# A linear-attention and mixture kernel: head work placed by a mask, key sums 64 columns wide, queries and first products in halves

## The chip, the cores and the metric

The kernel runs on one core of a Trainium2 chip. The metric is the device time of one execution in microseconds (us), the median over several runs. The engines are named as in the profile: PE is TensorE, PEld its weight loads, DVE VectorE, ACT ScalarE, POOL GpSimd, SP the engine that issues most DMAs.

## What is computed

Attention with a quadratic feature map, then a gated feed-forward (`_moe_ref`), then a soft mixture of 8 experts (`_moe2_ref`). The changed places serve the first two.

```python
def phi(x):                                   # S1, S2: 8 x 32
    a = np.einsum('rd,bhsd->bhsr', S1, x)
    b = np.einsum('rd,bhsd->bhsr', S2, x)
    return np.einsum('bhsi,bhsj->bhsij', a, b).reshape(*x.shape[:-1], r * r)
q_p, k_p = (phi(q), phi(k))                   # q, k, v: 4 x 4 x 1088 x 32
kv = np.einsum('bhsf,bhsd->bhfd', k_p, v)
z = np.sum(k_p, axis=2)
num = np.einsum('bhsf,bhfd->bhsd', q_p, kv)
den = np.einsum('bhsf,bhf->bhs', q_p, z)[..., None] + 1e-06
...
xn = x / rms * rms_g                          # 4352 tokens of 128
g = xn @ w_gate                               # 128 x 1536
val = xn @ w_val
return (silu * val @ w_out).astype(np.float32)
```

S1, S2 and the feed-forward weights arrive as 8-byte numbers. Each is made into a 4-byte word on the chip from its two halves (`f64_words`: two ACT passes, two DVE passes, one integer add).

## The kernel before

The tokens are worked off in nine tiles: tiles 0 to 7 hold 512 tokens, two for each batch, tile 8 the last 64 rows of all batches. For each tile the feed-forward runs through twelve slots (T, f), one for each 128 of the 1536 hidden columns. A slot's `ff_in` forms gate and value by three products each: high part of x by high part of the weight, high by low, low by high (`mm3`, lines 646 to 650), 512 tokens wide. ACT takes the silu of the gate (line 677), DVE multiplies it with the value (line 678), and two slots later `ff_out` adds the result to the tile's output. In tile 0 this last product uses whole 4-byte words (line 702), later tiles split words.

Before the first slot stands the head, which makes the sums of batch 0 and the x of tile 0. Its order is written out by hand in the string `FRONT` (lines 29 to 35), one token for one step; each engine keeps the order of the string. The tokens that matter here:

- `n:18` issues 18 products on constant data that nothing reads (line 301).
- `b` is `make_bd`: S1 and S2 become words, one PE transpose puts them on 128 partitions, and four ACT copies lay them into `bd`, a 128 x 64 block matrix with a 32 x 16 block for each head.
- `kt:g`, `kp:g`, `kx:g`, `ko:g` transpose the keys, multiply them with `bd`, copy one half of the result and form the outer products; `kv:hp` copies the values of two heads into `va`, 33 columns for each head and slice (32 values and a one).
- `ks:hp` sums outer products with values for the heads 2hp and 2hp+1 (line 389): 18 products with a stationary operand of 33 columns, the first head's at output partition 0, the second's at 64.
- `kw:hp` copies that sum to `kvT` (line 407, one copy for each head), `kb:hp` transposes it back, `kl:f` puts it in place (line 434).
- `qs`, `qp`, `qh`, `qo`, `qb`, `qa`, `qd` and so on do the same for the queries of tile 0; `qx` writes the high part of x (line 601), `ql` the low part (line 607).
- `c:i` is the next step of weight conversion i; i = 0, 1, 3, 4 hold gate and value columns for slots 0-1, 2-3, 4-5 and 6-7, i = 2 and 5 output weights. Line 192 and line 198 are its ACT passes, line 204 its add on POOL, line 242 the cast to the high part on ACT, line 249 the low part on POOL.

After the head the conversions go on beside the slots of tile 0. Batches 1 to 3 get their sums by `k_chain`, a step or two in each slot; the same line 389 works there. A scheduler that models the engines' times sets the order of the instructions from the first slots on, so any change in the head can reorder the rest. DMAs stand on SP's queue in the order in which the code issues them.

Of the kernel before, what the change touches and what calls it, by code (L numbers as in the profile page):

```python
# [8 lines left out]
F32 = mybir.dt.float32  # L9
F32R = mybir.dt.float32r  # L10
# [6 lines left out]
P = 128  # L17
# [13 lines left out]
FRONT = """  # L31
n:18 b n:5 kz kt:0 kt:1 qs kp:0 kp:1 kt:2 kx:0:a ko:0:d kx:1:b ko:1:p kc:2 qp kp:2 n:3 kv:0 kx:2:a ko:2:d qh kv:1 km
ks:0 c:0 qo:0 qo:1 qb c:0 c:0 ks:1 kw:0:a kb:0 kw:1:a n:4 kb:1 n:10 kl:0:a kl:1:d c:0 c:0 kr:a c:1
qa:0 qa:1 n:26 qd:0 qd:1 c:0 qq:0:a qq:1:d qq:2:a qq:3:d qr:0 qr:1 c:1 qm:0 qm:1 c:1 c:0 qt:0 qx:0 n:2 qt:1 qx:1 c:1 ql c:1 c:2 c:2 c:2
# [13 lines left out]
def body(ctx, tc, q, k, v, s1, s2, wg, wv, wo, rg, phi, w1, w2, out):  # L48
# [38 lines left out]
    kt, qt, kr, vt = {}, {}, {}, {}  # L87
    va = const.tile([P, H, 8, D1], F32, name="va")
    vr = const.tile([64, H, D1], F32, name="vr")

# [22 lines left out]
    def load_q(b):  # L113

        t = big("qt", 2)
        load(out=t.rearrange("p (h n) -> p h n", h=H), in_=q[b, :, 0:1024, :].rearrange("h (p j) d -> p h (j d)", j=8))
        qt[b] = t.rearrange("p (h j d) -> p h j d", h=H, j=8)

    stage = {}

# [18 lines left out]
    load_k(0)  # L139
    load_q(0)  # L140
    load_kr(0)
    load_v(0)
    load_w(w_keys[0])
    load_w(w_keys[1])
    g_sb = const.tile([P, 1], F32, name="g_sb")
# [18 lines left out]
    pool.memset(vr[:, :, D:D1], 1.0)  # L164
    mhalf = const.tile([P, 4], F32, name="mhalf")
# [20 lines left out]
    def f64_words(st, t, s, r, out):  # L186
# [14 lines left out]
        yield  # L201
        if len(out.shape) == 2:
            for c in cuts(out.shape[1]):
                mark["word"] = pool.tensor_tensor(out=out[:, c], in0=s[:, c], in1=r[:, c], op=ALU.add).ins
        else:
            s, r = (x.unsqueeze(1).to_broadcast(out.shape) for x in (s, r))
            pool.tensor_tensor(out=out, in0=s, in1=r, op=ALU.add)
        yield
# [51 lines left out]
    def make_bd():  # L260
        w = sb.tile([2 * R, D], F32, tag="cst", name="cst")
        s = sb.tile([2 * R, D], U32, tag="css", name="css")
        r = sb.tile([2 * R, D], U32, tag="csc", name="csc")
        w4 = sb.tile([2 * R, 4, D], F32, tag="csr", name="csr")
        for _ in f64_words(s64, w, s, r, w4.bitcast(U32)):
# [53 lines left out]
    class Keys:  # L319
# [58 lines left out]
        def sum(self, hp, ts, banks=1):  # L378

            for t in ts:  # L380
# [112 lines left out]
    class Queries:  # L493
# [389 lines left out]
    def front():  # L883
# [375 lines left out]
```

## Time and profile before

| What | us |
|---|---|
| Median of 3 runs (314.46 to 315.02) | 314.61 |
| Profiled execution, its own time | 314.55 |
| Span from first to last instruction | 312.8 |
| Part of its own time outside the span | 1.75 |
| PE busy | 303.6 |
| DVE busy | 234.5 |
| ACT busy | 181.7 |
| POOL busy | 63.4 |

The page of the profile gives busy time by engine and in 40 slices of 7.8 us. Finer questions are put to the trace: a timeline lists instructions in order of time, with the engine's idle time before one in brackets and what ended it, and windows give each engine's busy time in chosen stretches. Matmul records are pipelined and overlap; their durations are longer than the step from one to the next. The granted TensorE clock is 1.00 of full speed (2.4 GHz) in the stretches before 300 us.

### The profile page before, as it was taken

The page shows a single profiled execution, that of the slowest core. Times are in us where ns is not written, and L with a number is a line of the kernel's source. Part 1 is how long each engine was busy: PE and PEld are TensorE (multiplying, and loading weights), DVE is VectorE, ACT ScalarE, POOL GpSimd, SP SyncE. Part 2 cuts the span into 40 slices and gives each one's busy share as a digit, 9 for nine tenths or more (in the row PEclk, how much of TensorE's full clock was granted, in tenths as well). Part 3 has the DMA queues.
Part 4 walks back from the last instruction along what each step waited for, and adds up shares of the span by engine and source line. Part 5 has one row for each costly group of instructions (what it writes and reads, how often), then busy time and mean ns, then how long its engine had stood idle before and what let it go on. Part 6 is the DMA issues. An engine that isn't in the chain of part 4 may idle for free.

```text
span 312.8 us, 5555 instructions
## 1 busy us (share of the span) xinstructions
PE 303.6 (97%) x1977; PEld 241.8 (77%) x1977; DVE 234.5 (75%) x458; ACT 181.7 (58%) x411; POOL 63.4 (20%) x104
## 2 busy tenths in 40 slices
PE   8989999999999999999999999999999999999993
PEld 6776666778887878888888788888787778898482
DVE  4787967688789858967898689678787667666762
ACT  3768664455745467565544676555574655566552
POOL 3357998000612010020020100100020100003120
PEclk9999999999999999999999999999999999999999
DMA  8988000010035100010351000100891494000007
GB/s 204 311 300 216 0 0 1 11 25 2 0 112 111 25 2 0 11 25 0 91 130 25 3 0 9 26 0 10 290 266 26 129 303 106 2 0 2 3 32 254
DMA packets 44955, 23.97 MB, mean 77 GB/s; under 512 B 26880, under 2 KB 40960, under 8 KB 44928
## 3 DMA queue, kind: packets, MB, share of 16 engines
q1 hardware_dynamic: 44752, 23.56, 28.1%
q8 instruction: 15, 0.25, 0.3%
q10 hardware_dynamic: 176, 0.07, 0.1%
q14 instruction: 12, 0.10, 0.1%
HBM read 19.81 MB, written 2.23 MB: 70 GB/s over the span
## 4 chain that ended last, share of the span: by engine, by line
PE 87%; DVE 4%; SPq 2%; POOL 2%; ACT 2%; DMA 1%; issue 1%; DVEq 0%; POOLq 0%; ACTq 0%
PE v L647 8%; PE g L647 8%; PE g L649 8%; PE g L648 8%; PE v L648 7%; PE v L649 7%; PE o L649 7%; PE o L647 7%; PE o L648 7%; PE aux L534 4%; PE o L702 3%; PE aux L389 2%; SPq L76 2%; PE aux L359 2%; PE aux L511 2%; PE fo L1210 1%
## 5 line engine op out<-in xcount | busy, mean ns | idle before, releaser
L677 ACT ACTIVATE silu<-g 128x512 f32<-128x512 f32 (+1 forms) x103 | 60.5, 592 | 38.7 <-PE g L649 38.1
L687 ACT CAST hh<-hf 128x512 fp32r<-128x512 f32 x89 | 54.9, 617 | 44.4 <-DVE hf L678 42.8
L678 DVE TENSOR_TENSOR hf<-v,silu 128x512 f32<-128x512 f32 (+1 forms) x91 | 61.2, 677 | 23.4 <-ACT hh L687 7.8
L692 DVE TENSOR_TENSOR hl<-hf,hh 128x512 fp32r<-128x512 f32 x89 | 60.5, 682 | 13.6 <-ACT hh L687 12.6
L647 PE MATMUL g<-xh,wgh 128*128 128x512 f32 (+1 forms) x108 | 43.8, 407 | 1.0 <-ACT xh L601 0.6
L647 PE MATMUL v<-xh,wgh 128*128 128x512 f32 (+1 forms) x108 | 43.4, 402 | 0.0
L648 PE MATMUL g<-xh,wgl 128*128 128x512 f32 (+1 forms) x108 | 41.1, 380 | 0.5 <-POOL wgl L249 0.5
L649 PE MATMUL g<-xl,wgh 128*128 128x512 f32 (+1 forms) x108 | 41.5, 384 | 0.0
L648 PE MATMUL v<-xh,wgl 128*128 128x512 f32 (+1 forms) x108 | 41.4, 383 | 0.0
L649 PE MATMUL v<-xl,wgh 128*128 128x512 f32 (+1 forms) x108 | 40.9, 379 | 0.0
L647 PE MATMUL o<-hh,woh 128*128 128x512 f32 (+1 forms) x94 | 36.9, 393 | 0.0
L649 PE MATMUL o<-hl,woh 128*128 128x512 f32 (+1 forms) x94 | 36.8, 392 | 0.0
L648 PE MATMUL o<-hh,wol 128*128 128x512 f32 (+1 forms) x94 | 35.8, 381 | 0.0
L582 POOL TENSOR_SCALAR rs<-ss 128x4 f32<-128x4 f32 (+1 forms) x8 | 1.9, 241 | 142.9 <-ACT sq L575 142.9
L647 PEld LDWEIGHTS g<-xh,wgh 128*128 128x128 f32 x108 | 20.3, 188 | 6.6 <-ACT silu L677 1.5
L648 PEld LDWEIGHTS g<-xh,wgl 128*128 128x128 f32 x108 | 20.3, 188 | 4.9 <-POOL wgl L249 0.9
L647 PEld LDWEIGHTS v<-xh,wgh 128*128 128x128 f32 x108 | 20.4, 188 | 4.3 <-issue 1.1
L649 PEld LDWEIGHTS g<-xl,wgh 128*128 128x128 f32 x108 | 20.3, 188 | 4.0
L649 PEld LDWEIGHTS v<-xl,wgh 128*128 128x128 f32 x108 | 20.3, 188 | 4.0 <-issue 0.2
L648 PEld LDWEIGHTS v<-xh,wgl 128*128 128x128 f32 x108 | 20.4, 188 | 3.9 <-issue 0.7
L649 PEld LDWEIGHTS o<-hl,woh 128*128 128x128 f32 x94 | 17.7, 188 | 3.7 <-issue 0.8
L647 PEld LDWEIGHTS o<-hh,woh 128*128 128x128 f32 x94 | 17.7, 188 | 3.4 <-issue 0.4
(259 smaller groups left out, 510.7 us busy)
## 6 DMA issues: line engine op xcount, KB each, us to landing
ring<-in_moe_w_dram SPq DMA_DIRECT2D x12, 256.0 KB, 7.3
ring<-in_moe_w_dram SPq DMA_DIRECT2D x5, 512.0 KB, 5.3
ring<-in_k_dram SPq DMA_DIRECT2D x8, 256.0 KB, 2.9
qt<-in_q_dram SPq DMA_DIRECT2D x4, 512.0 KB, 5.3
ring<-in_v_dram SPq DMA_DIRECT2D x16, 128.0 KB, 4.6
ring<-in_moe_w_gate_dram SPq DMA_DIRECT2D x6, 256.0 KB, 6.3
ring<-in_moe_w_val_dram SPq DMA_DIRECT2D x6, 256.0 KB, 7.7
ring<-in_moe_w_out_dram SPq DMA_DIRECT2D x3, 512.0 KB, 7.1
```

Source lines behind the costliest of these rows:

```text
L76: i = (on or nc.sync).dma_start(out=out, in_=in_)
L359: pe.matmul(o, self.kT[g][:, P * t : P * t + pp], bdf, start=True, stop=True)
L389: pe.matmul(self.a["kv", hp][64 * h2 : 64 * h2 + D1, 64 * hp : 64 * hp + 64], va[:, h, 2 * i + g, :] if t < 8 else vr[:, h, :], self.pk[hp ...
L534: pe.matmul(o, pD[:, f, h, :], rhs, start=(f == 0), stop=(f == 1))
L647: first = pe.matmul(o, ah, bh, start=start, stop=False)
L648: pe.matmul(o, al, bh, start=False, stop=False)
L649: last = pe.matmul(o, ah, bl, start=False, stop=stop)
L677: mark["silu"] = act.activation(s[:, cs], g[:, cs], AF.Silu).ins
L678: mark["gate"] = mark["gate", T, f] = dve.tensor_tensor(out=hf32[T, f][:, cs], in0=v[:, cs], in1=s[:, cs], op=ALU.mult).ins
L687: act.copy(hh[T, f], hf32[T, f])
L692: dve.tensor_tensor(out=hl[T, f], in0=hf32.pop((T, f)), in1=hh[T, f].bitcast(F32), op=ALU.subtract)
L702: last = pe.matmul(ops[T][:, 0:w], w_c, h[:, cs], start=(c == 0), stop=(c == NF - 1))
```

## The change

In the head, four things are done otherwise, and `FRONT` is rewritten.

1. S is added up on DVE instead of POOL, and 16 x 32 instead of 16 x 128. Four small products put it on 128 partitions, and one DVE multiply with a mask `blk` lays it into `bd`. The four ACT copies and the transpose go.
2. The stationary operand of the sums is 64 columns wide instead of 33, so that it runs into the columns of the next slice or head. `kvT` is then written in one copy of 97 partitions for a pair of heads instead of two of 33. This holds for all batches.
3. Tile 0's queries are loaded by a DMA of their own, half as large; the other half follows behind the first pair of weights.
4. The first slot, (0, 0), forms its high products for tokens 0 to 255 first and 256 to 511 after.

```diff
 FRONT = """
-n:18 b n:5 kz kt:0 kt:1 qs kp:0 kp:1 ... kp:2 n:3 kv:0 kx:2:a ko:2:d qh kv:1 km
-ks:0 c:0 qo:0 qo:1 qb c:0 c:0 ks:1 kw:0:a kb:0 kw:1:a n:4 kb:1 n:10 kl:0:a kl:1:d c:0 c:0 kr:a c:1
+n:17 b n:5 kz kt:0 bm kt:1 qs kp:0 kp:1 ... kp:2 kv:0 kx:2:a ko:2:d qh kv:1 km
+ks:0 qo:0 qo:1 qb ks:1 kw:0:a c:0 c:0 kb:0 kw:1:a n:2 kb:1 n:10 kl:0:a kl:1:d c:0 c:0 c:0 kr:a c:1
...
@@ load_q
+        src = q[b, :, 0:1024, :].rearrange("h (p j) d -> p h (j d)", j=8)
+        if b > 0:
+            load(out=t, in_=src)
+        else:
+            q0 = row("hl", 3, F32R).bitcast(F32)
+            load(out=q0.rearrange("p (h n) -> p h n", h=H), in_=src[:, :, 0 : 4 * D])
+            q0s.append(q0)
+            return lambda: load(out=t[:, :, 4 * D :], in_=src[:, :, 4 * D :])
...
-    load_q(0)
+    rest_q = load_q(0)
     load_kr(0)
     load_v(0)
     load_w(w_keys[0])
+    rest_q()
     load_w(w_keys[1])
...
-    pool.memset(bd, 0.0)
+    blk = const.tile([P, H], F32, name="blk")
+    pool.memset(blk, 0.0)
+    for h in range(H):
+        pool.memset(blk[32 * h : 32 * h + 32, h : h + 1], 1.0)
...
-    pool.memset(kvT[32:64], 0.0)
...
@@ f64_words
+        if out.shape[1] == D:
+            dve.tensor_tensor(out=out, in0=s, in1=r, op=ALU.add)
...
@@ make_bd
-        pe.transpose(a[:, 0 : 2 * R], w4.rearrange("p h d -> p (h d)"), ident[0 : 2 * R, 0 : 2 * R])
-        for h in range(4):
-            act.copy(bd[32 * h : 32 * h + 32, h, :], a[32 * h : 32 * h + 32, 0 : 2 * R])
+        for h in range(H):
+            pe.matmul(a[32 * h : 32 * h + 32, 0 : 2 * R], w, ident[0 : 2 * R, 0 : 2 * R], start=True, stop=True)
+        kt["S"] = a
+
+    def place_bd():
+        a = kt.pop("S")[:, 0 : 2 * R].unsqueeze(1).to_broadcast([P, H, 2 * R])
+        dve.tensor_tensor(out=bd, in0=a, in1=blk.unsqueeze(2).to_broadcast([P, H, 2 * R]), op=ALU.mult)
...
@@ Keys.sum
+                    v0 = D1 * (8 * h + 2 * i + g) if t < 8 else D1 * h
                     pe.matmul(
-                        self.a["kv", hp][64 * h2 : 64 * h2 + D1, 64 * hp : 64 * hp + 64],
-                        va[:, h, 2 * i + g, :] if t < 8 else vr[:, h, :],
+                        self.a["kv", hp][64 * h2 : 64 * h2 + 64, 64 * hp : 64 * hp + 64],
+                        (va_all if t < 8 else vr_all)[:, v0 : v0 + 64],
...
@@ Keys.spread_1
-            for h2 in range(2):
-                r0 = 64 * h2
-                src = self.a["kv", hp][r0 : r0 + D1, 64 * hp : 64 * hp + 64].rearrange("p (a n) -> p a n", n=D)
-                eng(kvT[r0 : r0 + D1, 2 * hp : 2 * hp + 2], src.unsqueeze(2).to_broadcast([D1, 2, 4, D]))
+            src = self.a["kv", hp][0:97, 64 * hp : 64 * hp + 64].rearrange("p (a n) -> p a n", n=D)
+            eng(kvT[:, 2 * hp : 2 * hp + 2], src.unsqueeze(2).to_broadcast([97, 2, 4, D]))
...
@@ ff_in
+        if (T, f) == (0, 0):
+            os, sl = (gps[T, f][0], vps[T, f][0]), slice(0, P)
+            for cs in cuts(512):
+                for w_m in (wgh, wgl):
+                    for m, o in enumerate(os):
+                        last = pe.matmul(o[:, cs], w_m[:, m, sl], xh[T][:, cs], start=(w_m is wgh and cs.start == 0), stop=False)
+                        gate[0] = gate[0] or last.ins.name
+            for m, o in enumerate(os):
+                last = pe.matmul(o, wgh[:, m, sl], xl[T], start=False, stop=True)
+            mark["mm3"] = last.ins
+            return
```

`va_all` and `vr_all` are `va` and `vr` with 31 more columns, which POOL sets to zero; POOL also sets the mask, and no longer `bd` and the middle of `kvT`.

On DVE, at the start of the program, this stood between the words of S (`cst`, `css`) and the first outer products (`work`); `T` holds transposed keys, `x_192` the transposed queries:

```order
L194 TENSOR_SCALAR cst<-cst 16x32
L200 SCALAR_TENSOR_TENSOR css<-s_64,cst 16x32
L341 STREAM_TRANSPOSE T<-ring 128x2x4x32 x4
L506 STREAM_TRANSPOSE x_192<-qt 128x512
L287 TENSOR_TENSOR work<-asb,aux 128x1024
```

Now the add of S (a program's own instruction, shown as ISA, over 64 half words) and the multiply with the mask stand there too:

```order
L210 TENSOR_SCALAR cst<-cst 16x32
L216 SCALAR_TENSOR_TENSOR css<-s_64,cst 16x32
L219 ISA cst<-css,csc 16x64
L359 STREAM_TRANSPOSE T<-ring 128x2x4x32 x2
L288 TENSOR_TENSOR bd<-aux,blk 128x64
L359 STREAM_TRANSPOSE T<-ring 128x2x4x32 x2
L523 STREAM_TRANSPOSE x_198<-hl 128x512
L305 TENSOR_TENSOR work<-asb,aux 128x1024
```

The multiply has two of the four key transposes ahead of it and two behind.

On ACT, from the x of tile 0 on, the order was this; `silu_435`, `silu_465` and `silu_495` are the silus of slots 0, 1 and 2, `wgh<-cvt_321` is the cast of the gate and value columns for slots 2 and 3, and `hf`, `cvc` and `ring_407` belong to later conversions:

```order
L601 ACTIVATE xh_393<-v_398,g_sb_88 128x256
L192 ACTIVATE ring_407<-ring_90 128x512
L198 ACTIVATE cvc_409<-ring_90 128x512
L242 CAST wgh_133<-cvt_321 128x2x256
L677 ACTIVATE silu_435<-g_414 128x512
L192 ACTIVATE hf_445<-ring_92 128x512
L198 ACTIVATE cvc_447<-ring_92 128x512
L192 ACTIVATE hf_476<-ring_95 128x512
L677 ACTIVATE silu_465<-g_457 128x512
L677 ACTIVATE silu_495<-g_487 128x512
```

Now the same stretch reads so; `silu_438`, `silu_468` and `silu_498` are the silus of slots 0, 1 and 2, `wgh<-cvt_320` the cast for slots 2 and 3:

```order
L618 ACTIVATE xh_392<-v_397,g_sb_90 128x256
L208 ACTIVATE ring_406<-ring_92 128x512
L214 ACTIVATE cvc_408<-ring_92 128x512
L705 ACTIVATE silu_438<-g_413 128x512
L208 ACTIVATE hf_448<-ring_94 128x512
L208 ACTIVATE hf_479<-ring_97 128x512
L257 CAST wgh_141<-cvt_320 128x2x256
L214 ACTIVATE cvc_450<-ring_94 128x512
L705 ACTIVATE silu_468<-g_460 128x512
L214 ACTIVATE cvc_481<-ring_97 128x512
L300 COPY asb_484<-aux_455 128x128
L257 CAST wgh_141<-hf_448 128x2x256
```

The cast for slots 2 and 3 stood ahead of the first silu; it now stands behind that silu and two more passes.

On PE, slots 1 and 2 stood like this (`g_457` and `v_458` are slot 1, `g_487` and `v_488` slot 2):

```order
L647 MATMUL v_458<-xh_393,wgh_133 128x512
L648 MATMUL v_458<-xh_393,wgl_134 128x512
L649 MATMUL v_458<-xl_394,wgh_133 128x512
L647 MATMUL g_487<-xh_393,wgh_133 128x512
L648 MATMUL g_487<-xh_393,wgl_134 128x512
L649 MATMUL g_487<-xl_394,wgh_133 128x512
L647 MATMUL v_488<-xh_393,wgh_133 128x512
L648 MATMUL v_488<-xh_393,wgl_134 128x512
L649 MATMUL v_488<-xl_394,wgh_133 128x512
```

Now (`g_460`, `v_461` slot 1; `g_490`, `v_491` slot 2; `o_510` the tile's output):

```order
L664 MATMUL v_461<-xh_392,wgh_141 128x512
L665 MATMUL v_461<-xh_392,wgl_142 128x512
L666 MATMUL v_461<-xl_393,wgh_141 128x512
L664 MATMUL g_490<-xh_392,wgh_141 128x512
L664 MATMUL v_491<-xh_392,wgh_141 128x512
L730 MATMUL o_510<-hh_439,ring_406 128x512
```

Slot 2's products with the low weights now come later, behind the output products of slots 0 and 1.

## Rows read from the trace of the kernel before

**Rows 1.** The page, busy time of each engine (us, share of span, instructions):

```profile
PE 303.6 (97%) x1977; PEld 241.8 (77%) x1977; DVE 234.5 (75%) x458; ACT 181.7 (58%) x411; POOL 63.4 (20%) x104
```

**Rows 2.** Windows: length, then busy PE, PEld, DVE, ACT, POOL (instructions), clock, DMA:

```profile
22.06:25.10 3.04, 3.01 (x12) 2.17 (x12) 1.27 (x4) 2.22 (x5) 2.07 (x3) 1.00 0.33 98
25.10:27.28 2.18, 1.75 (x6) 0.97 (x6) 2.17 (x4) 2.18 (x5) 1.55 (x3) 1.00 0.88 278
27.28:33.60 6.32, 5.82 (x23) 3.64 (x23) 6.32 (x11) 4.79 (x10) 5.58 (x8) 1.00 0.62 136
33.60:42.55 8.95, 8.94 (x43) 6.81 (x44) 8.23 (x15) 6.03 (x11) 8.95 (x10) 1.00 0.00 0
100.00:150.00 50.00, 50.00 (x323) 40.67 (x322) 39.07 (x73) 28.95 (x68) 3.54 (x5) 1.00 0.07 11
```

**Rows 3.** Timeline, 4 to 7.7 us: start, us, instruction, [idle before <-releaser]:

```profile
4.34 0.18 DVE L200 SCALAR_TENSOR_TENSOR css<-s,cst 16x32 uint32<-16x32 uint32 x1
4.45 2.00 DVE L341 STREAM_TRANSPOSE T<-ring 128x256 f32<-128x256 f32 x4
4.67 0.44 POOL L207 TENSOR_TENSOR csr<-css,csc 16x128 uint32<-16x128 uint32 x1 [2.25 <-DVE css L200]
5.17 0.23 PE L268 MATMUL aux<-ident,csr 16*128 16x16 f32 x1
5.44 0.69 ACT L270 COPY bd<-aux 32x16 f32<-32x16 f32 x4 [1.22 <-PE aux L268]
6.18 1.10 PE L359 MATMUL aux<-bd,T 128*128 128x64 f32 x8
6.75 0.71 DVE L506 STREAM_TRANSPOSE x<-qt 128x512 f32<-128x512 f32 x1 [0.30 <-DMA qt<-in_q_dram]
```

**Rows 4.** Timeline, 9 to 14.2 us, key sums and their copies:

```profile
9.35 0.19 PEld L359 LDWEIGHTS g<-bd,T 128*64 128x64 f32 x2
9.61 0.50 PE L301 MATMUL idle<-hot 128*128 128x256 bf16 x3
9.95 0.62 ACT L352 COPY va<-ring 128x512 f32<-128x512 f32 x1
10.04 1.09 PE L389 MATMUL v<-work,va 128*33 128x64 f32 x32
12.31 0.30 PE L389 MATMUL aux<-pkr,vr 64*33 64x64 f32 x4
12.80 0.74 ACT L407 COPY kvT<-aux 33x256 f32<-33x256 f32 x2
13.60 0.30 PE L417 MATMUL aux<-ident,kvT 97*128 97x97 f32 x1
```

**Rows 5.** PE's weight loads, 239.87 to 239.90 us, where they are 64 columns wide:

```profile
239.88 0.15 PEld L541 LDWEIGHTS aux<-kvr,work 128*64 128x64 f32 x2 [0.35 <-issue]
```

**Rows 6.** Timeline, 21 to 27.4 us, the first slots:

```profile
21.54 0.48 ACT L601 ACTIVATE xh<-v,g_sb 128x256 fp32r<-128x256 f32 x1 [0.20 <-PE v L594]
22.07 0.50 PE L647 MATMUL g<-xh,wgh 128*128 128x512 f32 x1 [0.57 <-ACT xh L601]
22.30 1.63 POOL L204 TENSOR_TENSOR cvt<-cvs,cvc 128x256 uint32<-128x256 uint32 x2 [1.81 <-DVE cvs L200]
23.56 0.39 PE L649 MATMUL g<-xl,wgh 128*128 128x512 f32 x1
23.96 0.62 ACT L242 CAST wgh<-cvt 128x512 fp32r<-128x512 f32 x1 [0.82 <-POOL cvt L204]
24.48 0.59 ACT L677 ACTIVATE silu<-g 128x512 f32<-128x512 f32 x1
24.98 0.65 ACT L192 ACTIVATE hf<-ring 128x512 f32<-128x512 f32 x1
25.13 0.50 PE L647 MATMUL g<-xh,wgh 128*128 128x512 f32 x1
```

**Rows 7.** PE's timeline at 42.5 us, the first product of slot 8:

```profile
42.56 0.79 PE L647 MATMUL g<-xh,wgh 128*128 128x512 f32 x1
```

More of the change, by code (lines that the diff above doesn't have):

```diff
@@ L31 @@
 FRONT = """
-n:18 b n:5 kz kt:0 kt:1 qs kp:0 kp:1 kt:2 kx:0:a ko:0:d kx:1:b ko:1:p kc:2 qp kp:2 n:3 kv:0 kx:2:a ko:2:d qh kv:1 km
-ks:0 c:0 qo:0 qo:1 qb c:0 c:0 ks:1 kw:0:a kb:0 kw:1:a n:4 kb:1 n:10 kl:0:a kl:1:d c:0 c:0 kr:a c:1
+n:17 b n:5 kz kt:0 bm kt:1 qs kp:0 kp:1 kt:2 kx:0:a ko:0:d kx:1:b ko:1:p kc:2 qp kp:2 kv:0 kx:2:a ko:2:d qh kv:1 km
+ks:0 qo:0 qo:1 qb ks:1 kw:0:a c:0 c:0 kb:0 kw:1:a n:2 kb:1 n:10 kl:0:a kl:1:d c:0 c:0 c:0 kr:a c:1
 qa:0 qa:1 n:26 qd:0 qd:1 c:0 qq:0:a qq:1:d qq:2:a qq:3:d qr:0 qr:1 c:1 qm:0 qm:1 c:1 c:0 qt:0 qx:0 n:2 qt:1 qx:1 c:1 ql c:1 c:2 c:2 c:2
@@ L87, in body @@
     kt, qt, kr, vt = {}, {}, {}, {}
-    va = const.tile([P, H, 8, D1], F32, name="va")
-    vr = const.tile([64, H, D1], F32, name="vr")
+    va_all = const.tile([P, H * 8 * D1 + 31], F32, name="va")
+    vr_all = const.tile([64, H * D1 + 31], F32, name="vr")
+    va = va_all[:, 0 : H * 8 * D1].rearrange("p (h j d) -> p h j d", h=H, d=D1)
+    vr = vr_all[:, 0 : H * D1].rearrange("p (h d) -> p h d", d=D1)
     def load_k(b):
@@ L115, in load_q @@
         t = big("qt", 2)
-        load(out=t.rearrange("p (h n) -> p h n", h=H), in_=q[b, :, 0:1024, :].rearrange("h (p j) d -> p h (j d)", j=8))
         qt[b] = t.rearrange("p (h j d) -> p h j d", h=H, j=8)
+        src = q[b, :, 0:1024, :].rearrange("h (p j) d -> p h (j d)", j=8)
+        t = t.rearrange("p (h n) -> p h n", h=H)
+        if b > 0:
[5 more added lines that the diff above has]
+            return lambda: load(out=t[:, :, 4 * D :], in_=src[:, :, 4 * D :])
+    q0s = []
     stage = {}
@@ L161, in body @@
     bd = const.tile([P, H, 2 * R], F32, name="bd")
-    pool.memset(bd, 0.0)
+    blk = const.tile([P, H], F32, name="blk")
+    pool.memset(blk, 0.0)
+    for h in range(H):
+        pool.memset(blk[32 * h : 32 * h + 32, h : h + 1], 1.0)
     pool.memset(va[:, :, :, D:D1], 1.0)
     pool.memset(vr[:, :, D:D1], 1.0)
+    pool.memset(va_all[:, H * 8 * D1 :], 0.0)
+    pool.memset(vr_all[:, H * D1 :], 0.0)
     mhalf = const.tile([P, 4], F32, name="mhalf")
@@ L201, in f64_words @@
         yield
-        if len(out.shape) == 2:
+        if out.shape[1] == D:
+            dve.tensor_tensor(out=out, in0=s, in1=r, op=ALU.add)
+        else:
             for c in cuts(out.shape[1]):
                 mark["word"] = pool.tensor_tensor(out=out[:, c], in0=s[:, c], in1=r[:, c], op=ALU.add).ins
-        else:
-            s, r = (x.unsqueeze(1).to_broadcast(out.shape) for x in (s, r))
-            pool.tensor_tensor(out=out, in0=s, in1=r, op=ALU.add)
         yield
@@ L263, in make_bd @@
         r = sb.tile([2 * R, D], U32, tag="csc", name="csc")
-        w4 = sb.tile([2 * R, 4, D], F32, tag="csr", name="csr")
-        for _ in f64_words(s64, w, s, r, w4.bitcast(U32)):
+        for _ in f64_words(s64, w, s, r, w.bitcast(U32)):
             pass
         a = aux()
-        pe.transpose(a[:, 0 : 2 * R], w4.rearrange("p h d -> p (h d)"), ident[0 : 2 * R, 0 : 2 * R])
-        for h in range(4):
-            act.copy(bd[32 * h : 32 * h + 32, h, :], a[32 * h : 32 * h + 32, 0 : 2 * R])
+        for h in range(H):
[4 more added lines that the diff above has]
+        dve.tensor_tensor(out=bd, in0=a, in1=blk.unsqueeze(2).to_broadcast([P, H, 2 * R]), op=ALU.mult)
     bdf = bd.rearrange("p h r -> p (h r)")
@@ L397, in spread @@
         def spread(self):
-            for h2 in range(2):
-                r0 = 64 * h2
-                src = self.a["kv"][r0 : r0 + D1, 0:128].rearrange("p (a n) -> p a n", n=D)
-                act.copy(kvT[r0 : r0 + D1], src.unsqueeze(2).to_broadcast([D1, 4, 4, D]))
+            src = self.a["kv"][0:97, 0:128].rearrange("p (a n) -> p a n", n=D)
+            act.copy(kvT, src.unsqueeze(2).to_broadcast([97, 4, 4, D]))
         def spread_1(self, hp, eng):
-            for h2 in range(2):
-                r0 = 64 * h2
-                src = self.a["kv", hp][r0 : r0 + D1, 64 * hp : 64 * hp + 64].rearrange("p (a n) -> p a n", n=D)
-                eng(kvT[r0 : r0 + D1, 2 * hp : 2 * hp + 2], src.unsqueeze(2).to_broadcast([D1, 2, 4, D]))
+            src = self.a["kv", hp][0:97, 64 * hp : 64 * hp + 64].rearrange("p (a n) -> p a n", n=D)
+            eng(kvT[:, 2 * hp : 2 * hp + 2], src.unsqueeze(2).to_broadcast([97, 2, 4, D]))
         def back(self, ids=range(4), banks=1):
@@ L501, in shuffle @@
             self.qD = row("T", 2) if T else row("x2")
-            if T < 8:
+            if T == 0:
+                src = q0s[0]
+            elif T < 8:
                 src = qt[T // 2][:, :, 4 * (T % 2) : 4 * (T % 2) + 4, :].rearrange("p h j d -> p h (j d)")
@@ L893, in front @@
             "b": make_bd,
+            "bm": place_bd,
             "kz": k.zero,
```

## The prediction

> **What bounds the kernel now.** I read the page first: PE is busy for 97% of the span [rows 1]. Next come windows of the trace. In the steady part, 100 to 150 us, PE has no idle time at all, while DVE and ACT have a fifth or more of theirs free [rows 2]. So an edit that only relieves DVE, ACT or POOL there gives nothing; what counts is when PE's stream of slots begins, how much PE waits before it is closed up, and the length of PE's own work. The windows of the first slots show where it waits: 0.03, 0.43, 0.50 and 0.01 us from 22.06 to 42.55 us, 0.97 together, and nothing after [rows 2]. Last I read the timelines of the head and of the first slots, following what each instruction waited for [rows 3, 4, 6]. The head is a chain that passes through all engines: S, key projections, key sums, `kvT`, back transposes, queries, x of tile 0, first product at 22.07. The 1.75 us of the execution outside its span I leave as they are, so gains are taken from the profiled execution's 314.55; it lies 0.06 below the median of the runs, which is nothing at this size.
>
> **S and the mask.** Before, DVE's last word step ends at 4.52, POOL adds until 5.11, PE transposes, four ACT copies take 5.44 to 6.13, and the first projection starts at 6.18 [rows 3]. After, DVE adds by itself. No row shows that instruction; the step before it, 16 x 32, took 0.18 and POOL's add 0.44 [rows 3], so I bound it by these and take 0.2, since it has 64 columns on the engine of the 0.18. It ends at 4.75. PE's four small products follow in about 0.4 (the transpose took 0.23) beside two key transposes on DVE, half of the 2.00 for four; DVE starts each next instruction about 0.07 before the last ends (4.45 against 4.52) [rows 3], so they end near 5.7. Then the multiply: 64 columns from PSUM, not shown either; between 0.18 and the 0.69 of the four copies that it replaces, I take 0.22, nearer the single instruction. With 0.05 from the last copy to PE, as before, the first projection starts at 5.95, 0.23 earlier. With 0.44 and 0.69 it would start 0.5 later than this, 0.25 after the old time. What stands behind the multiply on DVE are two key transposes and that of the queries. The second half of the keys is wanted a projection later and is there in time. The queries' transpose waited 0.30 for its DMA [rows 3]; with half the bytes in front of it that wait goes, and it pays for the 0.42 of the two new DVE instructions. The outer products of the keys thus start about 0.1 earlier, and PE's projections, which run back to back, 0.23 earlier.
>
> The POOL memsets and SP's one more DMA issue cost nothing that I can find: POOL has 2 us free before 4.67 [rows 3]. The second half of the queries stands in SP's queue ahead of the second pair of weights and all later ones, but the bytes ahead of these are the same as before, and an issue takes under half a us; only tile 1 wants that half. If the cover failed, the cost would be that issue.
>
> **Key sums.** Before, three idle products stand at 9.61 and the first sum starts at 10.04 [rows 4]. Without them it starts behind the last projection (9.35 less 0.23), at about 9.28. A new wait appears: the last slice of head 1, read 64 columns wide, runs into the first slice of head 2, which the second `va` copy writes. That copy ended at 10.57 [rows 4] and ends near 10.35 now; the last products of the first sum wait 0.25 for it, and behind them on PE stand the rest of this sum and the second one. Both sums took from 10.04 to 12.61 [rows 4], so now 9.28 + 2.57 + 0.25 = 12.10. Then `kvT`: two copies ended at 13.54, at 0.37 each and behind two conversion passes on ACT [rows 4]. One copy of the same columns ends at 12.5, and one of the passes has moved behind the next placing copies. The second back transpose starts at 12.56 instead of 13.60: **1.04 earlier**. Placing, attend, divide and x follow in the same order with the same waits, so I carry 1.04 to the first slot. The moved ACT pass runs while DVE still prepares the other operand of POOL's add.
>
> Width costs PE itself nothing if the two heads' loads still run side by side. The sums' step is 1.09 less one record for 32, 56 ns for a pair [rows 4]. Elsewhere in this trace two 64-wide loads at different output partitions take 0.15 together, against 0.19 for two in one place [rows 4, 5], so they overlap and the load hides under the product. I take 0. The other end is no overlap at all, a pair taking twice its step, 56 ns more: 18 pairs in each of eight sums (two in each batch), 1.0 us a sum, 8 in all. A page of the Trainium skill leans that way: "TensorE: Matmul & The Clock Gate", section LDWEIGHTS, has a load's time grow with its columns, by its rate an estimate of 27 ns for 33 columns and 53 for 64, so 107 for two one after another. Against it, "TensorEngine Tiling (Array Packing)", Key Properties, has tiles load and multiply in parallel; the 64-wide loads here agree with that, 0.15 for two.
>
> **First slot.** PE waited 0.57 for the second half of x [rows 6]. Now four half products, 256 columns, fit into that gap. A product takes about 0.25 (12 in 3.01) [rows 2]; I cost a half at 0.12, bounded by 0.25 if halving saved nothing, which would cost 0.5 more. Lead of PE at the end of slot 1: 1.04 + 0.46 = **1.5**, at about 23.55 instead of 25.08.
>
> **What is given back.** This is the step that I trust least and that decides. Slot 2's gate needs the cast of its weights on ACT. Before, that cast stood ahead of the first silu, and PE went on at 25.13 with almost no stop [rows 6]. Now it stands behind the first silu and two passes. The silu waits for the low product of the gate (23.56 less 1.5, plus 0.4 for its run): 22.5. From the silu's start to the next pass is 0.50 [rows 6], the two passes take about 0.55 each, the cast 0.62: done at 24.75, PE at 24.8. PE has run out at 23.55 and stands for 1.25. The lead falls to 0.33. But the work that before stood behind later waits now comes first: two high products, an output product, the projection for tile 1. Of the old waits, 0.43 and 0.50, I find about 0.15 (the first output product waits for POOL's add, which waits for the multiply of slot 0) and 0.25 (slot 4's gate waits for the silu of slot 2, now behind another cast). So 0.33 + 0.93 - 0.40 = 0.86, less some 0.05 for the restarts: the lead at slot 8, at 42.56 before [rows 7], is **0.8**. POOL and DVE are full there, 8.95 and 8.23 of 8.95 us [rows 2], but their chains start over a us earlier too, and each low part comes 0.6 or more before PE wants it. After that PE is closed up, and the reordered steady part changes nothing that I can price.
>
> Sum: 314.55 - 0.8 = 313.75; I say **313.8**.
>
> **Rivals.**
> - The gain is kept. If ACT's cast came as early as before relative to PE, nothing would be given back and 1.5 remain: 313.05. For it: the waits of 0.43 and 0.50 that exist now also absorb. Against: in-order ACT and the order shown.
> - The change doesn't move the end. The conversions set PE's pace until slot 8: POOL is busy for all of 33.60 to 42.55 [rows 2]. POOL's low part for slot 2 now stands behind an add that waits for slot 0's product. If another us is lost there, the lead is gone: 314.55, up to 315.2 if the conversions come out later than before. Against: POOL's chain has idle time ahead of it (1.81 at 22.30 [rows 6]), which moves up.
> - Slower: the 64-wide loads do not overlap in the sums. At 56 ns a pair 2 us in the head and 6 us in the chains of batches 1 to 3, where PE has no idle time: 314.55 - 0.8 + 8 = 321.7. From 10 ns a pair on, 1.4 us over the 144 pairs, the change is slower by over 0.2%. Against: the overlap at 239.88 [rows 5]. For it: there the products are twice as long, so the load has more cover.
>
> **Numbers.** Runs of this kernel spread by about 0.2%, 0.6 us, so that is the bound for no change: 313.98 to 315.24. Forecast, 313.3 to 314.3: 0.46. Gain kept, 312.6 to 313.3: 0.17. No effect, 314.3 to 315.3: 0.27. Slower by wide loads: 0.10. Faster takes the second and 0.40 of the first, 0.57; same takes 0.06 and 0.23, 0.29; slower 0.04 and 0.10, 0.14. The range for 8 in 10 is 312.8 to 315.2; the forecast's own is 313.3 to 314.3. It holds the unknown terms: the S instructions' 0.5, the half products' 0.5.
>
> **What would show it.** In the changed profile: first projection near 5.95; a stop of about 0.25 inside the first sum; second back transpose near 12.56; first half product near 20.5; a stop of PE near 23.5 that the cast ends, over 1 us long; PE's step in the sums still 56 ns a pair; slot 8's first product near 41.75; no PE idle from there to the tail. The forecast is wrong if that stop is missing, if a later stop appears between slots 4 and 8, or if the sums in the three later chains grow.

## The result, and the profile after

The changed kernel takes 316.48 us (median of 6 runs, 315.73 to 316.77), the kernel before 314.59 beside it (6 runs, 314.45 to 315.02). The ratio is 1.0056, with a 95% interval of 1.0043 to 1.0069: slower, by 1.9 us, where 313.8 was forecast. The span of the profiled execution is 314.7 us against 312.8. The page of the changed kernel, busy time of each engine, answers to [rows 1]; PE again has 97%:

```profile
PE 304.2 (97%) x1982; PEld 243.1 (77%) x1982; DVE 234.7 (75%) x460; ACT 179.9 (57%) x402; POOL 61.8 (20%) x108
```

Windows of the changed kernel (columns as in [rows 2]): the first slots, cut where PE stops, a stretch near 95 us, and the steady part:

```profile
20.00:25.43 5.43, 4.22 (x22) 2.99 (x22) 4.45 (x10) 4.36 (x9) 1.88 (x4) 1.00 0.92 293
25.43:27.83 2.40, 2.40 (x12) 1.59 (x13) 2.26 (x4) 1.69 (x3) 2.40 (x4) 1.00 1.07 259
27.83:31.82 3.99, 3.39 (x14) 2.16 (x14) 3.95 (x6) 1.44 (x4) 3.99 (x5) 1.00 0.24 47
31.82:40.98 9.16, 9.16 (x43) 6.88 (x44) 8.98 (x18) 7.84 (x18) 8.47 (x11) 1.00 0.00 0
91.00:97.00 6.00, 5.00 (x24) 3.77 (x23) 6.00 (x11) 4.41 (x9) 0.00 (x0) 1.00 0.94 250
100.00:150.00 50.00, 50.00 (x323) 41.06 (x322) 38.82 (x72) 29.70 (x68) 3.35 (x5) 1.00 0.07 11
```

PE stands 1.2 us in the first of these, 0.6 in the third, and a whole microsecond between 91 and 97 us. In the kernel before, PE had no idle time there:

```profile
91.00:97.00 6.00, 6.00 (x32) 4.83 (x31) 6.00 (x11) 4.62 (x10) 0.00 (x0) 1.00 0.99 266
```

From 100 to 150 us PE is full, as before; how long the products in a full window take, no window tells.

The head, in the timeline of the changed kernel (answers to [rows 3] and [rows 4]; start, us, instruction, idle before and what ended it). First S and the mask:

```profile
4.43 0.18 DVE L219 CUSTOM_DVE_ANT_0 cst<-css,csc 16x64 uint16<-16x64 uint16 x1
4.96 0.30 PE L283 MATMUL aux<-ident,cst 16*32 16x16 f32 x8
5.20 1.07 PE L319 MATMUL idle<-hot 128*128 128x256 bf16 x5
5.47 0.19 DVE L288 TENSOR_TENSOR bd<-aux,blk 128x64 f32<-128x64 f32 x1
6.10 1.00 PE L377 MATMUL aux<-bd,T 128*128 128x64 f32 x8
```

`bd` is ready at 5.66, but PE begins the projection at 6.10, without any wait: five products on constant data (`n:5`) stand ahead of it. Then the sums:

```profile
9.29 1.49 PE L408 MATMUL v<-work,va 128*64 128x64 f32 x31
10.97 1.15 PE L408 MATMUL aux<-work,va 128*64 128x64 f32 x32
12.05 0.33 PE L408 MATMUL aux<-pkr,vr 64*64 64x64 f32 x4
12.43 0.37 ACT L422 COPY kvT<-aux 97x256 f32<-97x256 f32 x1 [0.37 <-PE aux L408]
12.85 0.30 PE L432 MATMUL aux<-ident,kvT 97*128 97x97 f32 x1
```

And the first slots (answers to [rows 6] and [rows 7]):

```profile
20.94 0.39 PE L689 MATMUL g<-xh,wgh 128*128 128x256 f32 x1
21.84 1.62 POOL L222 TENSOR_TENSOR cvt<-cvs,cvc 128x256 uint32<-128x256 uint32 x2 [1.81 <-DVE cvs L216]
22.19 0.45 PE L664 MATMUL g<-xh,wgh 128*128 128x512 f32 x1
23.15 0.60 ACT L705 ACTIVATE silu<-g 128x512 f32<-128x512 f32 x1 [0.45 <-PE g L692]
23.64 1.23 ACT L208 ACTIVATE hf<-ring 128x512 f32<-128x512 f32 x2
24.75 0.62 ACT L257 CAST wgh<-cvt 128x512 fp32r<-128x512 f32 x1
25.43 0.50 PE L664 MATMUL g<-xh,wgh 128*128 128x512 f32 x1 [1.17 <-ACT wgh L257]
```

The cast's operand is done on POOL at 23.46; the cast starts at 24.75, behind the silu and two passes. The first product of slot 8 starts at 42.27. The last product of its value, first in the changed kernel and then in the kernel before:

```profile
43.82 0.39 PE L666 MATMUL v<-xl,wgh 128*128 128x512 f32 x1
44.81 0.40 PE L649 MATMUL v<-xl,wgh 128*128 128x512 f32 x1
```

It is done at 44.21, before at 45.21. But before, three products of slot 9's gate (0.68) had been done by then too, so by equal work PE leads by only 0.31 us there. All the loss comes after it. Two stops are seen at once, in the timeline near 92 and 96 us (SPq is the queue's own row):

```profile
91.04 0.66 SPq L76 DMA_DIRECT2D kr<-in_k_dram  x1
92.06 0.50 PE L664 MATMUL g<-xh,wgh 128*128 128x512 f32 x1 [0.25 <-ACT silu L705]
96.67 0.24 PE L362 MATMUL aux<-ident,kr 64*128 64x64 f32 x1 [0.75 <-DMA kr<-in_k_dram]
```

`kr`, the last 64 keys of batch 2, is waited for: the new order of the steady part asks for it right behind the projection of the first keys. Before, it was issued at nearly the same time, but its reader stood behind the whole projection and three products more:

```profile
91.12 0.66 SPq L76 DMA_DIRECT2D kr<-in_k_dram  x1
96.57 0.27 PE L344 MATMUL aux<-ident,kr 64*128 64x64 f32 x1
```

In the changed kernel PE is free for it at 95.92, 0.65 earlier, and the transfer lands at 96.54, 5.5 us after its issue.

The rest I found by the distance between starts, which I call the step. From one 512-column product of high and low parts to the next (pairs in which the second starts before the first ends, under 260 ns) the mean is 228.50 ns before (682 steps) and 229.85 in the changed kernel (699 steps): 1.35 by 699 is 0.94 us, spread over the program. In settled rows, runs of such products without another kind between them, the step is mostly 226 or 227 in both kernels. Steps of 229 to 259, nearly all of them up to 236, are 179 of 702 behind 45 us before, and 362 of 715 after. In the changed kernel a row of two or more settled steps goes over into longer ones 22 times without another kind of product between, and each time the longer step begins with a product that reads `hl`; before, this never happens. The rows of the product of h's low part show it in the median (durations, min/median/max; 389 belongs to the short step), first the changed kernel:

```profile
L666 PE MATMUL v<-xl,wgh x107: 278/389/485, 23.9 to 285.3; 128*128 128x512 f32 x95, 128*128 128x256 f32 x12
L666 PE MATMUL o<-hl,woh x94: 277/394/502, 63.2 to 286.5; 128*128 128x512 f32 x84, 128*128 128x256 f32 x10
```

and the kernel before:

```profile
L649 PE MATMUL o<-hl,woh x94: 278/389/499, 65.1 to 284.9; 128*128 128x512 f32 x84, 128*128 128x256 f32 x10
```

### The profile page after: what moved, and what is told of

Its sections match the earlier page's. It is cut to its first block, busy times and chain, and to the rows that moved or that the text cites. A ratio compares the mean times of both kernels' runs of the same rounds, so it can differ in the third digit from the quotient of the medians.

```text
span 314.7 us, 5571 instructions
## 1 busy us (share of the span) xinstructions
PE 304.2 (97%) x1982; PEld 243.1 (77%) x1982; DVE 234.7 (75%) x460; ACT 179.9 (57%) x402; POOL 61.8 (20%) x108
## 4 chain that ended last, share of the span: by engine, by line
PE 88%; DVE 4%; POOL 2%; DMA 2%; issue 1%; ACT 1%; SPq 0%; DVEq 0%; POOLq 0%; ACTq 0%
PE v L664 7%; PE g L664 7%; PE g L665 7%; PE v L665 7%; PE g L666 7%; PE v L666 7%; PE o L666 7%; PE o L664 7%; PE o L665 6%; PE aux L551 4%; PE o L730 3%; PE aux L408 3%; PE aux L377 2%; PE aux L528 2%; DMA kr<-in_k_dram 2%; PE idle L319 2%
## 5 line engine op out<-in xcount | busy, mean ns | idle before, releaser
L664 PE MATMUL g<-xh,wgh 128*128 128x512 f32 (+1 forms) x107 | 44.7, 418 | 2.0 <-ACT wgh L257 1.2
L664 PE MATMUL v<-xh,wgh 128*128 128x512 f32 (+1 forms) x107 | 42.0, 393 | 0.0
L666 PE MATMUL g<-xl,wgh 128*128 128x512 f32 (+1 forms) x107 | 40.6, 379 | 0.0
```

Source lines behind the costliest of these rows:

```text
L664: first = pe.matmul(o, ah, bh, start=start, stop=False)
L666: last = pe.matmul(o, ah, bl, start=False, stop=stop)
```

## The experiments

All ratios are to the kernel before, run beside them on the same chip; the 95% interval stands in brackets behind a ratio. The changed kernel itself has 1.0056 (1.0043 to 1.0069). The edits are shortened; `...` marks what is left out.

**The two kinds of stop.** `e1_cast_first` sets the cast directly behind the first silu, and the later conversion passes behind the cast (`mark["pace"]`):

```diff
-        with tc.issue_after(mark["silu"]) if kind == "o" else nullcontext():
-            act.copy(dh, src)
+        with tc.issue_after(mark["silu"]) if kind == "o" or i == 1 else nullcontext():
+            c = act.copy(dh, src)
+        if key == ("gv", 1):
+            mark["pace"] = c.ins
```

> The changed kernel, with one order set on ACT: the cast of the second weights pair follows the first silu directly, ahead of the two passes on hf. Theory A (the stop of 1.17 us before slot 2 is made by ACT's order, since the sum that the cast reads is done on POOL at 23.46): the stop shrinks to 0.1 to 0.2, and of the 1.0 some part is given back at the next old wait (0.60 at 31.2); 315.5 to 316.0 us. Rival B (the conversions on POOL and DVE set PE's pace until slot 8): the stop goes, the same microsecond stands later before slot 8, and the time stays at 316.4 within 0.3.

Measured 316.59 us, 1.0056 (1.0043 to 1.0068): no gain. The order is as asked; ACT's timeline:

```profile
23.63 0.60 ACT L707 ACTIVATE silu<-g 128x512 f32<-128x512 f32 x1 [0.45 <-PE g L694]
24.12 0.61 ACT L257 CAST wgh<-cvt 128x512 fp32r<-128x512 f32 x1
```

and of PE's stops 0.84 us are left up to slot 8, instead of 1.76; those at 92 and 96 are gone as well, in another order of the steady part. Windows of this run, 25 to 45 and 45 to 290 us:

```profile
25.00:45.00 20.00, 19.19 (x79) 12.49 (x79) 17.95 (x30) 14.20 (x31) 19.25 (x23) 1.00 0.24 57
45.00:290.00 245.00, 245.00 (x1482) 199.17 (x1480) 186.37 (x342) 138.93 (x307) 29.89 (x53) 1.00 0.22 56
```

So neither theory holds as put: 1.9 us of idle time went and the time stayed. PE's rows are broken more often here: 70 product steps are longer than 260 ns, 57 in the changed kernel. Such a step (mostly the first behind another kind of product) is 0.31 to 0.34 us instead of 0.23, so 13 more cost 1.0 to 1.4 us. The first slot of this profile began 0.48 later besides, which needn't be an effect of the edit: with one order the start of the first slot differs that much between profiles (20.91 to 21.55 in the four with the changed kernel's order, 21.91 to 22.64 in the seven with the order of before). That the broken rows are what costs the gain is argued, not shown.

`e2_keys_rest_early` issues `kr` ahead of the queries:

```diff
             load_k(b)
-            load_q(b)
             load_kr(b)
+            load_q(b)
```

> The changed kernel, with the load of the last 64 keys (kr) issued ahead of the queries' in batches 1 to 3. Theory A (the stop of 0.75 us at 95.92 is kr's transfer, wanted earlier in the new order of the steady part): no stop there, 315.6 to 315.9 us. Rival B (PE there waits for whatever was loaded last, the queries or values then): a stop of the same kind moves to the next transfer and the time stays at 316.4 within 0.3.

Measured 315.85, 1.0031 (1.0020 to 1.0042), by the ratios 0.8 us less: theory A. `kr` is issued at 90.46, and its reader on PE starts without a stop; the 0.25 that waits for the silu stays:

```profile
95.79 0.27 PE L362 MATMUL aux<-ident,kr 64*128 64x64 f32 x1
```

PE's order is that of the changed kernel up to 158 us, and so the stop near 96 us is compared at equal order; behind that the scheduler orders it anew.

**Parts undone.** `e3_narrow_sums`: `va` and `vr` read 33 columns wide, two copies into `kvT`:

```diff
-                        (va_all if t < 8 else vr_all)[:, v0 : v0 + 64],
+                        (va_all if t < 8 else vr_all)[:, v0 : v0 + D1],
...
```

> The changed kernel with 33 columns in the key sums and two copies into kvT, as before, everything else kept. Theory A (a wide load costs 2 to 5 ns a pair, 0.5 us in the three later chains, and 0.24 in the stop inside the first sum, against one more copy of 0.37 in the head): step of a pair back from 58 to 56 ns, time lower by 0.2 to 0.6, 315.9 to 316.3 us, apart from what the other order of the steady part does to the stops at 91.8 and 95.9. Rival B (width is free and the copies are what counts): 316.5 to 317.0 us.

Measured 316.37, 1.0049 (1.0035 to 1.0062); the 0.2 us to the changed kernel lies within the intervals. This total doesn't price the width: PE's order is another from the first sum on, and the stop for `kr` is 0.16 here instead of 0.75. The traces are plainer. One sum of batch 3 in the changed kernel:

```profile
174.21 1.15 PE L408 MATMUL aux<-work,va 128*64 128x64 f32 x32
175.29 0.50 PE L664 MATMUL v<-xh,wgh 128*128 128x512 f32 x1
176.65 0.33 PE L408 MATMUL aux<-pkr,vr 64*64 64x64 f32 x4
176.91 1.15 PE L408 MATMUL aux<-work,va 128*64 128x64 f32 x32
```

and with narrow loads:

```profile
173.14 1.09 PE L409 MATMUL aux<-work,va 128*33 128x64 f32 x32
174.16 0.50 PE L669 MATMUL v<-xh,wgh 128*128 128x512 f32 x1
175.97 0.30 PE L409 MATMUL aux<-pkr,vr 64*33 64x64 f32 x4
176.21 1.09 PE L409 MATMUL aux<-work,va 128*33 128x64 f32 x32
```

1.08 against 1.02 and 0.26 against 0.24: 0.08 a sum, about 0.5 us in the six later ones. The two copies in the head cost nothing visible: the first slot begins at 20.81 instead of 20.94, within the spread given at `e1`.

`e4_whole_first_slot` takes the half products out:

```diff
-        if (T, f) == (0, 0):
-            ...
-            return
```

> The changed kernel with the first slot's products over whole 512-column tiles, as before. Theory A (eight half products cost 0.3 us more than four whole ones, and save the wait for the second half of x, 0.57 before; what they save is lost at the cast's stop): first product 0.5 later, the stop before slot 2 about 0.5 shorter or gone, time 316.0 to 316.6 us. Rival B (the half products' lead reaches the end): 316.9 to 317.2 us.

Measured 316.09, 1.0039 (1.0026 to 1.0051), in theory A's range. The first product is at 21.54, the stop of 1.17 is gone, and PE stands 0.95 us in the slots. But this run alone doesn't refute rival B: in its order the stops near 92 and 96 us are gone too, 1.0 us, and that could hide a loss of the half products' lead. `e18` below, compared with `e16`, has only 0.27 us of such a difference.

**Where the operands lie.** The change moves tensors in SBUF. `va` and `vr` grow, and `hl`, used for the queries in the head, is laid out early, at byte 148,608 of a partition instead of 220,320. First I moved all tensors together, by 288 bytes in the kernel before (`e5`), 224 in the changed kernel (`e6`), and 32 and 64 in the kernel before (`e7`, `e8`):

```diff
+    const.tile([P, n // 4], F32, name="shift")      # n bytes that nothing reads
```

> The kernel before, with one more tensor of 288 bytes that nothing reads behind va, so that the weights, x and h stand where the change put them modulo 512 bytes; every engine's order is that of before. Theory A (the step of one 512-column product to the next, 228.5 ns on average before and 229.9 in the changed kernel, follows where the operands stand in SBUF): step up by 1.2 to 1.5 ns, time up by 1.0 to 1.3 us, 315.6 to 315.9 us where before stands at 314.6. Rival B (the step follows the order of the products, or something else of the change): no change within 0.3 us.

> The changed kernel, with one more tensor of 224 bytes that nothing reads, so that the weights, x and hh stand again where they stood before modulo 512 bytes (hl doesn't: it lies 192 bytes further in that measure); every engine's order is that of the changed kernel. Theory A (place in SBUF sets the step of the products): step from 229.9 to 228.5 to 229.0 ns, time lower by 0.7 to 1.2 us, 315.3 to 315.8. Rival B: 316.2 to 316.8 us.

> The kernel before, with an unread tensor of 32 bytes: operands of the products at 0 instead of 32 modulo 64 bytes. Theory A1 (what counts is the place modulo 64): as with 288 bytes, 1.0 to 1.3 us slower. Theory A2 (what counts is a larger stretch, or where single tensors lie to each other, which this keeps): within 0.3 us of before. Rival B (place has no part): within 0.3 us of before, as all the shifted ones.

> The kernel before, with an unread tensor of 64 bytes: operands of the products still at 32 modulo 64 bytes. Theory A1 (place modulo 64): within 0.3 us of before, step 228.5 ns. If this one is slower by 1 us too while the one of 32 is not, the measure is another one than 64 bytes.

Measured: 0.9991 (0.9979 to 1.0004) with 288 bytes, 1.0005 (0.9991 to 1.0019) with 32, 1.0000 (0.9990 to 1.0010) with 64, the step 228.6 ns in all three; the changed kernel with 224 bytes 1.0051 (1.0038 to 1.0064), step 229.7. Theory A fell: a common shift does nothing. What was left was `hl` against the others. The next two, `e9` and `e10`, ask for buffers without using them, and every engine's order remains that of the kernel they start from (shortened):

```diff
+            row("hl", 3, F32R)                               # e10, in the kernel before
+            for tag, bufs, w in (("work", 4, 1024), ...):    # e9, ahead of hl in the changed kernel
+                sb.tile([P, w], F32, tag=tag, name=tag, bufs=bufs)
```

> The changed kernel with the buffers' places in SBUF asked for in the order of before, so that hl lies behind hf again, at 219,520 instead of 148,608, and kvz, work, T, x and hh within 500 bytes of their places before; every engine's order is that of the changed kernel. In the changed kernel each longer step that follows a settled stretch of 227 ns begins with a product that reads hl, in before none does. Theory C (the step depends on where hl lies to the other operands): step from 229.9 to 228.4 to 228.7 ns, time lower by 0.8 to 1.2 us, 315.2 to 315.7. Rival D (the step goes with the order of the products, whatever their places): 229.7 to 230.0 ns and 316.2 to 316.8 us.

> The kernel before with hl placed early in SBUF, at 148,320 instead of 220,320, as the change does; every engine's order is that of before. Theory C: step from 228.5 to 229.6 to 230.1 ns, time up by 0.8 to 1.3 us, 315.4 to 315.9 us where before stands at 314.6 (316.0 where it stands at 314.9). Rival D: 228.4 to 228.7 ns, time as before.

`e10`, `hl` early in the kernel before: 315.83 us, 1.0033 (1.0020 to 1.0045), step 229.95, and 26 settled rows that break off at `hl`: theory C, to the size. Its row has the median of the changed kernel:

```profile
L651 PE MATMUL o<-hl,woh x94: 277/394/505, 65.0 to 285.8; 128*128 128x512 f32 x84, 128*128 128x256 f32 x10
```

`e9`, `hl` late in the changed kernel: 318.51, 1.0119 (1.0105 to 1.0132), 2.0 us slower still, step 233.2, where C had promised a gain. Its row for the product that reads x's low part, which the place of `hl` shouldn't touch:

```profile
L673 PE MATMUL v<-xl,wgh x107: 276/394/475, 24.5 to 287.7; 128*128 128x512 f32 x95, 128*128 128x256 f32 x12
```

I had kept x and h within 500 bytes of their old places but not their distance to the weights. In this run every moving operand begins 448 bytes past the weights, modulo 512; in the changed kernel only `hl` is off, by 192; before, all begin at the same residue. Two more runs, `e11` and `e12`, were planned together with `e9` and share its layout and its step, 233.3 ns:

> The changed kernel with three things mended: hl placed as before, the last 64 keys loaded ahead of the queries in batches 1 to 3, sums 33 columns wide again with two copies into kvT. If the terms found so far add up (hl 1.0, the stop at 95.9 0.75, width 0.3 net): 316.5 - 2.0 = 314.3 to 314.7 us, level with or 0.3 below the kernel before. If the place of hl has no part: 315.2 to 315.6 us.

> The same three things mended, and the cast of the second weights pair right behind the first silu on ACT. If the 1.2 us stop before slot 2 is worth anything once PE isn't held elsewhere: 0.3 to 0.9 us below the kernel with three things mended, 313.5 to 314.3 us. If what is saved there goes into interrupted rows of products, as the run with the cast alone suggests: level with it within 0.3 us.

They took 317.49 (1.0090, 1.0076 to 1.0103) and 317.54 (1.0086, 1.0073 to 1.0100). Then the residue itself, with gaps of 320 bytes ahead of and 192 behind `hl` in the changed kernel, or of n bytes between the weights and all that moves past them in the kernel before:

```diff
+            sb.tile([P, 80], F32, tag="gap", name="gap")       # e13
             q0 = row("hl", 3, F32R).bitcast(F32)
+            sb.tile([P, 48], F32, tag="gap2", name="gap2")
+    sb.tile([P, n // 4], F32, tag="gap", name="gap")           # e14 (64), e15 (256)
```

> The changed kernel with 320 unread bytes ahead of hl and 192 behind it: hl stays early in SBUF, at 148,928, but begins at the weights' address modulo 512 bytes, as x and hh do; orders as in the changed kernel. Theory C1 (the step is short where the moving operand and the weights begin at the same place modulo 512, or a part of it): no longer steps begin at hl, 229.9 to 228.5 to 228.8 ns, time lower by 0.8 to 1.2 us, 315.2 to 315.7. Rival C2 (hl's region in SBUF counts): 229.6 to 230.1 ns, 316.2 to 316.8 us.

> The kernel before with 64 unread bytes between the weights and all that moves past them (x, h): order as before, 64 bytes of difference modulo 512. Theory C1: step from 228.5 to about 233 ns, as in the run whose difference was 448, over some 830 products: 3.5 to 4.0 us slower, 318.2 to 318.8. Rival C2: as before within 0.3 us.

> The same with 256 bytes. If the measure is 512 bytes: about 233 ns, 3.5 to 4 us slower. If it is 64, 128 or 256 bytes: 228.4 to 228.7 ns and as before within 0.3 us. Rival C2: as before.

`e13`, `hl` aligned and still early: 315.27, 1.0015 (1.0004 to 1.0025), by the ratios 1.3 us less than the changed kernel with the same order on every engine; step 228.6, and no settled row breaks off at `hl` any more. Some 0.3 of the 1.3 is not the step: `kr`'s stop has 0.46 in this profile,

```profile
96.22 0.24 PE L364 MATMUL aux<-ident,kr 64*128 64x64 f32 x1 [0.46 <-DMA kr<-in_k_dram]
```

and with the same order 0.58 in `e6`, 0.31 in `e9` and 0.75 in the changed kernel. `e14`, the kernel before with 64 bytes: 1.0027 (1.0016 to 1.0038), slower by 0.8 rather than 3.5, step 229.6. `e15`, with 256: 1.0002 (0.9993 to 1.0011), step 228.5. The rows of `e13`, `e14` and `e15`, in this order:

```profile
L668 PE MATMUL o<-hl,woh x94: 278/389/500, 63.2 to 285.4; 128*128 128x512 f32 x84, 128*128 128x256 f32 x10
```

```profile
L650 PE MATMUL o<-hl,woh x94: 279/392/503, 65.2 to 285.9; 128*128 128x512 f32 x84, 128*128 128x256 f32 x10
```

```profile
L650 PE MATMUL o<-hl,woh x94: 278/389/499, 64.9 to 284.8; 128*128 128x512 f32 x84, 128*128 128x256 f32 x10
```

**All terms together.** `e16` has `hl` aligned, `kr` early and narrow sums; `e17` adds the cast behind the silu, `e18` instead the whole first slot:

> The changed kernel with three things mended: hl aligned with the weights modulo 512 bytes, the last 64 keys loaded ahead of the queries in batches 1 to 3, sums 33 columns wide with two copies into kvT. If the terms add up (1.0 for hl, 0.75 for the wait at 95.9, 0.2 to 0.3 for the width): 314.3 to 314.7 us, level with the kernel before; taken from the run with two of them mended, whose step was 233.3 ns (317.5 us, less 830 products by 4.8 ns): 313.5 us, 0.3 to 0.5% faster than before. Rival C2: 315.3 to 315.8 us.

> The mended kernel (hl aligned, keys' rest early, narrow sums) with the cast of the second weights pair right behind the first silu. If the stop of 1.16 us before slot 2 is worth its length: 313.1 to 313.6 us. If the waits that it replaces come back as a row of interrupted products and later stops, as in the run with the cast alone: 314.0 to 314.4 us, level with the mended kernel.

> The mended kernel with the first slot's products over whole tiles. If the half products' lead only fills the stop before slot 2, and each costs 0.04 us more than half a whole one: 0.0 to 0.4 us lower than the mended kernel, 313.8 to 314.2. If the lead of the half products reaches the end: 314.5 to 314.8 us.

`e16` took 314.21, 0.9977 (0.9966 to 0.9988): the change pays once these three are mended, by 0.7 us. `e17` 314.26, 0.9981 (0.9972 to 0.9990): no gain from the stop is seen here either. `e18` 313.93, 0.9971 (0.9961 to 0.9981), the lowest of all. Its interval overlaps that of `e16`, and the stop of 0.27 near 91 us that `e16` still has is gone in it; so the half products show neither a gain nor a cost. What is left of the change in it is S on DVE, the one multiply, the split load of the queries and the order of the head.

## Why the prediction was wrong

**The step that failed** is the last of its working: "After that PE is closed up, and the reordered steady part changes nothing that I can price." From slot 8 to the end the kernel loses 2.2 us by the spans (0.31 ahead to 1.9 behind), and the runs name the terms: `kr`'s transfer 0.75 by the trace and 0.8 by `e2`; the place of `hl` 0.94 by the steps and 1.3 by `e13`, 0.3 of which is the shorter stop for `kr` there; the wider loads 0.5 by the traces; 0.25 behind a silu and 0.12 in the tail, which no run took away by itself. That is 2.6 by the traces. The 0.4 that this is too much I can't place (the order has fewer broken rows, 57 against 67, which points that way).

Point by point:

- **S and the mask.** The instructions cost what was taken, 0.18 and 0.19. The projection came at 6.10 instead of 5.95, a lead of 0.08: the keep-busy products, which I left out of the chain, hold PE until then. In this profile `bd` was ready 0.4 us earlier than PE could use it. The working also mis-added its bad case: 0.24 and 0.47 above the two estimates are 0.7 us, not 0.5; it didn't come to that.
- **Sums.** Start 9.18, one product ahead of the row shown (9.28 forecast). The stop inside the first is there, a step of 0.24 for one of 0.06. Both ended at 12.38 instead of 12.10. "Width costs PE itself nothing" was mis-sized: in the later chains it cost 0.08 a sum. The rival built on no overlap is refuted: a pair steps on every 58 ns instead of 56, not every 112, though each load takes 138 ns. The trace agrees with the Trainium skill, "TensorEngine Tiling (Array Packing)", Key Properties, which has different tiles load and multiply in parallel. The load itself grew from 111 to 138 ns for 31 columns more; by the rate in the Trainium skill, "TensorE: Matmul & The Clock Gate", section LDWEIGHTS, I estimate 26 ns for these, which is close to the 27 here.
- **Back transpose and x.** 12.85, not 12.56: 0.75 of lead for 1.04. x was waited for by 0.68 (0.38 before), since POOL's two power steps took 1.63 for 1.40.
- **First slot.** First half product at 20.94, a lead of 1.13 for the 1.6 that a product at 20.46 would have had. A half cost 0.156 (eight in 1.25), not 0.12: 0.3 more.
- **The give-back.** Right in place and cause, a stop of PE that the cast ends. Its length, 1.17 us for 1.25, came right because both of its ends moved: PE ran out at 24.26 instead of 23.55 and went on at 25.43 instead of 24.8. Behind both stand the slips above; the silu that the cast waits behind started at 23.15 instead of 22.5. One old wait of 0.60 remained, for a forecast 0.40. By slot 8 the lead was 0.31 for 0.8. These slips alone would have left the forecast's direction, about 314.3 us.
- **Rivals.** "Slower" came true, but not by its mechanism: the loads overlap, and the wider ones cost 0.5 us, not 6, in the later chains. Of the three signs of being wrong one came, the sums in the later chains grew. "A later stop appears" was named only up to slot 8, and the two stops came at 92 and 96 us, against "no PE idle from there to the tail".

## What to carry to other kernels

Where PE is full, a change in the head is paid for in the steady part: compare not only idle time but the step from product to product, as the median duration of each product's row shows it. A change that adds or moves a buffer is also a change of layout: look where the moving operands begin against the weights, modulo 256 bytes, before crediting or blaming anything else. And a reordered program wants its loads checked again one by one: a transfer with little to spare is no longer hidden when its reader moves up by a few products. In the kernel before, `kr` of batch 3 landed at 159.34 and was wanted at 159.47; that of batch 2 had its reader moved up by 0.65 us, and PE stood 0.75.

## What the hardware showed

The step of a 512-column product of split words depends on where its moving operand and the weights begin in SBUF, to each other. Means of the steps under 260 ns, worked out from the starts (the residues from the addresses of the built kernels):

| Moving operand less weights, modulo 512 bytes | Step, ns | Kernels |
|---|---|---|
| 0 for all | 228.3 to 228.6 | before, e5, e7, e8, e13, e16, e17, e18 |
| 256 for all | 228.5 | e15 |
| 64 for all | 229.6 | e14 |
| 192 for `hl`, 0 for x and hh | 229.7 to 230.1 | changed, e1 to e4, e6, e10 |
| 448 for all | 233.2 to 233.3 | e9, e11, e12 |

0 and 256 are alike, and in the runs with only `hl` off, the step from its product to the next has 232.2 to 232.7 ns on average. So the measure is 256 bytes or a part of it. A part such as 128 or 64 doesn't fit: 64 and 448 lie 384 bytes apart, a multiple of both, and have 229.6 and 233.2 ns. (Their orders differ too, but with all operands at 0 the orders differ by no more than 0.3 ns.) A difference of 128 itself wasn't tried. While one product reads its moving operand, the weights of the next are loaded (a load starts some 224 to 234 ns ahead of its product and takes 188), so two reads of SBUF go on at once. That they get in each other's way by place would explain the step; no run here shows it. A common shift of 32, 64 or 288 bytes changes nothing.
